# A one-core decode block: query table by a VectorE transpose, softmax sums by one product, the output weights loaded in another partition order

## The chip, the cores and the metric

The kernel runs on one core of one Trainium2 chip. The metric is the device time of one execution in microseconds (us); lower is better. The kernel before has a median of 1302.57 us in 3 runs (1302.52 to 1302.81).

## The reference: what is computed

One decode step of a block with attention and a feed-forward part side by side, all in float32: 4 sequences, one new token each, 32 heads of 128, 4096 cached keys and values per head, width 512, inner width 1792.

```python
xn = _layernorm(x)                                  # x: 4 x 1 x 512
q = (xn @ wq)                                       # 4 sequences, 32 heads, 128
scores = einsum("bhqd,bhkd->bhqk", q, k_cache) * 128 ** -0.5
o = einsum("bhqk,bhkd->bhqd", softmax(scores), v_cache)
out = x + o.reshape(4, 1, 4096) @ wo + silu(xn @ w1) @ w2
```

The two caches hold 268 MB each, so 561 MB are read from memory for a few thousand numbers of output.

## The kernel before

**Loads.** All large loads are issued by SyncE (SP) and go through one queue, in the order of the program: w1, wq, then k and v alternately, then wo in two halves and w2 in five pieces (function `load`, L161 to L165; issues L168 to L323). Only x (by ScalarE, L169) and the result (L527) go through another queue. There are three large buffers in SBUF of 64 KB per partition: `kb[0]`, `kb[1]` and `vb`. The keys of a step go to `kb[0]` and `kb[1]` in turn, the values to `vb`. The early weights lie in buffers that are not yet needed: w1 and the work space of the layer norm in `kb[1]`, wq in `vb`. At the end wo lies in `vb` and w2 in `kb[1]`. SP waits before an issue until the buffer is free: `k_free` comes from ScalarE when it has read the scores of a step, `v_free` from TensorE when it has collected the output of a step.

**Start.** VectorE computes the layer norm over the 4 rows of x (L190 to L219). TensorE transposes the result into `xpad` (L252), multiplies it with w1 (L259) and, when wq has landed, with wq (L273). The 4 column groups of TensorE work at the same time; each computes the queries of 8 heads for 4 sequences, with 32 output rows of which 4 are used. The query table `q_col` holds for each of the 32 steps (one sequence, 4 heads) a column of 128 numbers per head. It is made by scaling `ps_q` into `q_all` (L279), 32 products with a selection matrix `heads` (L286) and a copy (L295). The first load of v needs the buffer of wq and waits for the products with wq (`p_q`, L306).

**Steps.** 32 steps, two per loop iteration (L342 to L432). In each, VectorE multiplies the keys with the query (L358), GpSimd and VectorE add up the products (L378, L353), ScalarE takes the exponentials (L390) and leaves their sums per partition in `sums`, TensorE multiplies the weights with the values (L408) and collects the output into `o_t` (L419).

**End.** With the last step done, VectorE spreads `sums` over a selection matrix `quad` (L444), four products with `ones` give the softmax sums (L455), their reciprocals are taken (L461), `o_t` is transposed in blocks (L464), a product with the permutation `perm` puts rows in the order of wo (L468), and the result is scaled into `xo` (L474). Then come 32 products with wo (L487), one for each of the 32 rows that a partition holds, and 7 with w2 (L493), all into `ow`, again with 4 column groups; ScalarE copies `ow` to `os` (L498). Four more rows of w2 are multiplied with another arrangement (`accumulate`, L237 to L243: the 512 output columns are cut into 4 blocks of 128, one for each column group, into `acc`), then `os` is added to `acc` by a product with `pick` (L505), then two rows of w2, then the last row in two halves (L508 to L525). The input x had been added to `acc` by products at the start (L247). The result goes out by L527.

wo is loaded with `wo.rearrange("(p r) n -> p r n")`: partition p gets rows 32 p to 32 p + 31, the first 16 of them by the first load and the others by the second.

## Time and profile before

| | |
|---|---|
| median of 3 runs | 1302.57 us |
| the profiled execution: its own time | 1303.4 us |
| the profiled execution: span from first to last instruction | 1300.5 us |
| bytes moved by DMA | 561.07 MB, mean 431 GB/s |
| busy: VectorE 964.9, GpSimd 580.9, TensorE 361.1, ScalarE 110.2 us | 74%, 45%, 28%, 8% of the span |
| mean granted TensorE clock | 0.623 |

In the rows of the profile, L12 is line 12 of the kernel. DVE is VectorE, PE is TensorE's products and PEld its weight loads, ACT is ScalarE, POOL is GpSimd, SP is SyncE, and a name with a q (SPq) is that engine's sequencer. A row of the timeline has the start in us, the busy time in us, engine, line, operation, output and input, and the number of instructions merged in it; in brackets stands how long the engine was idle before it and what ended that. The tiles that share a buffer are shown under the buffer's name, `k` for `kb[0]` and `kb[1]` and `v` for `vb`, so w1 and w2 land in `k` and wq and wo in `v`. A float32 product is carried out as two passes and counts two records.

### The profile page before, as it was taken

What the parts mean: (1) busy time and instruction counts of PE and PEld (TensorE: products, weight loads), DVE (VectorE), ACT (ScalarE), POOL (GpSimd) and SP (SyncE); (2) the same over time, 40 slices, a digit from 0 to 9 for tenths busy, and PEclk for the clock granted to TensorE, in tenths of its full rate; (3) what the DMA queues carried; (4) which work ended last, traced back from release to release, by engine and by line L of the source; (5) the groups of instructions that cost most, each with busy time, mean ns of one, the idle gap of its engine ahead of it and who ended that gap; (6) DMA issues with size and microseconds to landing.
All of it is one profiled execution on the core that took longest, in us unless ns stands there. A gap on an engine that the chain in (4) does not pass through costs nothing. (4 is left out here: it accounts for less than half of the span.)

```text
span 1300.5 us, 7378 instructions
## 1 busy us (share of the span) xinstructions
PE 361.1 (28%) x2628; PEld 113.3 (9%) x2628; DVE 964.9 (74%) x449; ACT 110.2 (8%) x311; POOL 580.9 (45%) x137
## 2 busy tenths in 40 slices
PE   2221233321233221123322132332123332113337
PEld 0100001000000000000000000100000000001002
DVE  2499877887777887777797777788777788777770
ACT  1010101001010100101000010100101010010100
POOL 0255534554444554443555443455444455444350
PEclk8755666655666655666665566665566665566668
DMA  9999999999999999999999999999999999999998
GB/s 403 450 422 440 429 441 427 435 435 423 447 423 447 423 445 425 441 429 439 427 437 433 425 445 423 447 423 447 423 443 427 439 429 441 427 431 439 423 433 358
DMA packets 10533, 561.07 MB, mean 431 GB/s; under 512 B 1176, under 2 KB 1432, under 8 KB 1568
## 3 DMA queue, kind: packets, MB, share of 16 engines
q1 hardware_dynamic: 10512, 560.99, 99.6%
q8 instruction: 3, 0.05, 0.0%
q10 hardware_dynamic: 16, 0.02, 0.0%
q14 instruction: 2, 0.02, 0.0%
HBM read 561.00 MB, written 0.01 MB: 431 GB/s over the span
## 5 line engine op out<-in xcount | busy, mean ns | idle before, releaser
L378 POOL TENSOR_TENSOR k<-k 128x2048 f32<-128x2048 f32 x128 | 578.7, 4532 | 676.8 <-POOLq L326 676.8
L358 DVE TENSOR_TENSOR k<-k,q_b 128x4096 f32<-128x4096 f32 x128 | 562.4, 4414 | 226.2 <-DVEq L326 226.1
L408 PE MATMUL o_ps<-v,p_t 128*16 128x512 f32 x1984 | 285.0, 739 | 867.1 <-PEq L326 867.1
L353 DVE TENSOR_REDUCE s<-k 128x32 f32<-128x2048 f32 x128 | 290.8, 2272 | 17.9 <-DVEq L326 17.9
L408 PEld LDWEIGHTS o_ps<-v,p_t 128*16 128x16 f32 x1984 | 67.1, 113 | 1059.2 <-issue 1059.2
L398 ACT ACTIVATE o_sb<-o_ps 128x512 f32<-128x512 f32 x32 | 19.1, 597 | 1010.2 <-ACTq L326 1010.2
L329 DVE COPY q_of<-q_col 128x4 f32 (+1 forms) x33 | 84.8, 2571 | 0.0
L390 ACT ACTIVATE p_t<-s,gm 32x128 f32<-32x128 f32 x128 | 65.9, 515 | 46.0 <-ACTq L326 43.9
L419 PE MATMUL o_t<-pick,o_sb 128*128 128x4 f32 x256 | 33.6, 254 | 33.3 <-PEq L326 33.3
L419 PEld LDWEIGHTS o_t<-pick,o_sb 128*128 128x128 f32 x256 | 31.0, 191 | 62.6 <-issue 62.6
L390 ACT ACT_TABLE_LOAD x16 | 20.5, 1283 | 98.4 <-ACTq L326 98.4
L390 ACT ACTIVATION_READ_ACCUMULATOR p_t<-s,gm x128 | 24.9, 195 | 0.0
L279 DVE TENSOR_SCALAR q_all<-ps_q 128x1024 f32<-128x1024 f32 x1 | 1.2, 1224 | 20.6 <-PE ps_q L273 20.6
L444 DVE TENSOR_TENSOR k<-sums,quad 128x512 f32<-128x512 f32 x1 | 0.7, 693 | 19.0 <-PE o_t L419 19.0
L333 DVE STREAM_TRANSPOSE q_b<-q_of 128x128 f32<-128x128 f32 x33 | 10.8, 327 | 4.9
L367 DVE TENSOR_REDUCE m<-s 128x1 f32<-128x128 f32 x32 | 9.2, 286 | 4.7
L273 PE MATMUL ps_q<-v,xpad 128*32 128x512 f32 x64 | 8.8, 706 | 13.3 <-DMA v<-in_A_wq_dram 13.3
L408 PE MATMUL o_ps<-k,p_t 128*16 128x512 f32 x64 | 9.5, 757 | 8.3 <-DMA k<-in_A_v_cache_dram 8.3
L369 DVE STREAM_TRANSPOSE mt<-m 128x32 f32<-128x32 f32 x32 | 6.8, 212 | 4.7
L522 DVE COPY k<-acc 4x128 f32<-4x128 f32 x2 | 0.6, 286 | 12.5 <-PE acc L239 12.5
L371 DVE TENSOR_REDUCE gm<-mt 128x1 f32<-128x32 f32 x32 | 6.0, 186 | 4.7
L267 DVE STREAM_TRANSPOSE hT<-k 128x448 f32<-128x448 f32 x1 | 0.9, 939 | 10.3 <-ACT k L265 10.3
(62 smaller groups left out, 54.1 us busy)
## 6 DMA issues: line engine op xcount, KB each, us to landing
v<-in_A_wo_dram SPq DMA_DIRECT2D x2, 4096.0 KB, 27.2
k<-in_B_w_dram SPq DMA_DIRECT2D x1, 3584.0 KB, 11.2
k<-in_B_w_dram SPq DMA_DIRECT2D x1, 1792.0 KB, 30.3
k<-in_B_w_dram SPq DMA_DIRECT2D x1, 1024.0 KB, 32.4
k<-in_A_k_cache_dram SPq DMA_DIRECT2D x32, 45.4
k<-in_B_w_dram SPq DMA_DIRECT2D x1, 512.0 KB, 33.2
v<-in_A_v_cache_dram SPq DMA_DIRECT2D x31, 27.2
k<-in_B_w_dram SPq DMA_DIRECT2D x2, 128.0 KB, 33.0
```

The source lines that it names most:

```text
L273: t = nc.tensor.matmul(ps_q[32 * j : 32 * j + 32, u, :], xpad[:, c, :], wq_t[:, c, h * Dh : (h + G) * Dh], start=(c == 0), stop=(c == DC - 1),
L329: nc.vector.tensor_copy(q_of, q_col[:, at, :].rearrange("p i g -> p (i g)")).then_inc(spread_done, 1)
L333: nc.vector.transpose(q_b[:, n, :], q_of[:, :, None].to_broadcast([P, G, PH])).then_inc(spread_done, 1)
L353: nc.vector.tensor_reduce(s[:, a:z], k[:, a:z, : Dh // 2], axis=AX, op=ALU.add).then_inc(summed, 1)
L358: nc.vector.tensor_tensor(k[:, a:z, :], k[:, a:z, :], q_b[:, n, None, :].to_broadcast([P, z - a, Dh]), op=ALU.mult,).then_inc(products, 1)
L367: nc.vector.tensor_reduce(m_t, s, axis=AX, op=ALU.min).then_inc(summed, 1)
L369: nc.vector.transpose(mt, m_t.to_broadcast([P, PH])).then_inc(summed, 1)
L378: nc.gpsimd.tensor_tensor(kb[n][:, a:z, : Dh // 2], kb[n][:, a:z, : Dh // 2], kb[n][:, a:z, Dh // 2 :], op=ALU.add,).then_inc(halves, 1)
L390: t = nc.scalar.activation(p_t[rows, :, g], s_t[n][rows, :], AF.Exp, bias=gm[n][rows, :], scale=-1.0, accum_out=sums[rows, bass.ds(i * 2 + ...
L398: nc.scalar.activation(o_sb.rearrange("p r d -> p (r d)"), o_ps, AF.Copy).then_inc(rows_ready, 1)
L408: t = nc.tensor.matmul(o_ps[j : j + NR * G, :], p_t[:, rows, :].rearrange("p r g -> p (r g)"), v[:, rows, :].rearrange("p r d -> p (r d)") ...
L419: t = nc.tensor.matmul(to, o_sb[:, r, :], pick[:, r * G : (r + 1) * G], start=(r == 0), stop=(r == NR - 1),)
```

## The change

1. **Query table.** The products with wq are arranged so that column group j computes head 4 n + j, and not 8 j + n: only the columns of `wq_t` that a product takes change. One VectorE transpose in blocks of 32 x 32 takes `ps_q` (128 x 1024) to `q_t`, which lies in `vb` over wq, and one VectorE instruction scales it into `q_col`. `q_all`, `heads` and their 32 products are gone. The first load of v now waits for `d_col`, since `q_t` is in its buffer.
2. **Softmax sums.** `lt` is 128 x 128 instead of 128 x 512, `ones` is 128 x 128, and one product gives every sum in the place where `o_t` has the number to be divided. VectorE takes the reciprocal, multiplies, and transposes into `xo`. The product with `perm` is gone, and so is the clearing of `xo`.
3. **wo.** The transpose leaves the heads in another order over the partitions. wo is loaded in that order: partition 32 q + h gets rows 128 h + 32 q to 128 h + 32 q + 31. Each partition still gets 16 rows of 512 by the first load and 16 by the second, and each is one run of 32 KB in memory. The products take 4 columns of `xo` and not 32.
4. **x.** x lies in rows 8 to 11 of a cleared tile of 32 rows, `x_sb`; its load waits for the clearing. The layer norm is over 32 rows. Before the steps, VectorE copies `x_sb` into the first 32 rows of `ow` and clears the others; `add_x` takes rows 8 to 11 with the sums. The 4 products that added x to `acc` are gone.
5. **w2.** 12 rows instead of 7 go into `ow`; the copy `os` is after all of these; one row is left for `acc`, then `os`, then the last row. The second load of w2 has 5 rows and not 4, the third 1 and not 2.

```diff
-W2_CUTS = (7, 11)
+W2_CUTS = (7, 12)
+X_ROW = 8
...
-        got_x = load(act, "x", x_sb, xf)
+        c_x = dve.done(nc.vector.memset(x_sb, 0.0))
+        got_x = load(act, "x", x_sb[X_ROW : X_ROW + B], xf, c_x)
...
-        pe.wait(c_ident, got_x)
-        accumulate(ident[:B, :B], x_sb, start=True)
...
+        wq_g = wq_t.rearrange("p c (n g d) -> p c n g d", g=G, d=Dh)
...
-                        wq_t[:, c, h * Dh : (h + G) * Dh], start=(c == 0), stop=(c == DC - 1),
+                        wq_g[:, c, G * u : G * u + G, j, :], start=(c == 0), stop=(c == DC - 1),
...
-        d_q = dve.done(nc.vector.tensor_scalar_mul(
-                q_all.rearrange("p u g d -> p (u g d)"), ps_q.rearrange("p u n -> p (u n)"), -scale,
-            ))
-        pe.wait(d_q, d_pick)
-        for g in range(G):
-            for a in range(4):
-                for u in range(NQ):
-                    t = nc.tensor.matmul(
-                        ps_b[32 * g : 32 * g + 32, 32 * a : 32 * a + 32],
...
+        d_qt = dve.done(
+            nc.vector.transpose(q_t, ps_q.rearrange("p u (m e) -> p (u m) e", e=PH))
+        )
+        dve.wait(d_qt)
         d_col = dve.done(
-            nc.vector.tensor_copy(q_col[:, :T, :], ps_b.rearrange("p (a i) -> p i a", a=4))
-        )
+            nc.vector.tensor_scalar_mul(
+                q_col[:, :T, :].rearrange("p (n b) a -> p n b a", b=B),
+                q_t.rearrange("p (n a) e -> p n e a", a=G)[:, :, :B, :], -scale,
+            )
+        )
+
+        nc.vector.tensor_copy(ow[:PH], x_sb)
+        nc.vector.memset(ow[PH : 2 * PH], 0.0)
+        d_ow = dve.done(nc.vector.memset(ow[2 * PH :], 0.0))
...
-            load(sp, "v", vb, cache(v_cache, i), p_q if i == 0 else (v_free, i))
+            load(sp, "v", vb, cache(v_cache, i), d_col if i == 0 else (v_free, i))
...
-        wo_p = wo.rearrange("(p r) n -> p r n", p=P)
+        wo_p = wo.rearrange("(h q r) n -> q h r n", q=4, r=PH)
...
-            got_wo.append(load(sp, name, wo_t[:, a:z], wo_p[:, a:z], (v_free, T - 1)))
+            got_wo.append(load(sp, name, wo_t[:, a:z], wo_p[:, :, a:z], (v_free, T - 1)))
...
+        p_l = pe.done(
+            nc.tensor.matmul(
+                ps_b, ones, lt.rearrange("p t g -> p (t g)"), start=True, stop=True
+            )
+        )
         dve.wait(p_l)
...
+        t = dve.done(nc.vector.reciprocal(rl.rearrange("p t g -> p (t g)"), ps_b))
+        dve.wait(t, p_o)
+        t = dve.done(nc.vector.tensor_tensor(o_n, o_t, rl, op=ALU.mult))
+        dve.wait(t)
         d_x = dve.done(
...
+            nc.vector.transpose(xo, o_n.rearrange("p (n b) g -> p b n g", b=B))
+        )
...
-                    ow[j : j + 32, :], xo[:, r, :], wo_t[:, r, :], start=(r < 4), stop=False
+                    ow[j : j + B, :], xo[:, :, r], wo_t[:, r, :], start=(r < 4), stop=False
...
+        rows = f_edges[-2]
+        for n, (a, z) in enumerate(zip(f_edges[:-2], f_edges[1:-1])):
+            pe.wait(got_w2[n])
+            for f in range(a, z):
+                j = 32 * (f % 4)
+                t = nc.tensor.matmul(
+                    ow[j : j + B, :], hT[:, f, :B], w2_t[:, f, :], start=False,
+                    stop=(f >= rows - 4),
+                )
         act.wait(pe.done(t))
         a_os = act.done(nc.scalar.activation(os, ow, AF.Copy))
...
+        pe.wait(got_w2[-1])
+        for f in range(rows, f_edges[-1]):
+            accumulate(hT[:, f, :B], w2_t[:, f, :], start=(f == rows))
+        pe.wait(a_os, d_add)
+        accumulate(add_x, os)
```

Three places in the order of the instructions. First SP at the end of its program, behind the last load of keys or values; `k` and `v` are the buffers, and the shape is that of the destination, partitions first. Before:

```order
L163 DMA k_90<-in_A_v_cache_dram 128x16384
L163 DMA v<-in_A_wo_dram 128x8192 x2
L163 DMA k_91<-in_B_w_dram 128x3584
L163 DMA k_91<-in_B_w_dram 128x2048
L163 DMA k_91<-in_B_w_dram 128x1024
L163 DMA k_91<-in_B_w_dram 128x256 x2
```

In the change:

```order
L164 DMA k_88<-in_A_v_cache_dram 128x16384
L164 DMA v<-in_A_wo_dram 128x1x8192 x2
L164 DMA k_89<-in_B_w_dram 128x3584
L164 DMA k_89<-in_B_w_dram 128x2560
L164 DMA k_89<-in_B_w_dram 128x512
L164 DMA k_89<-in_B_w_dram 128x256 x2
```

The order of the loads is the same; the two loads of wo have a dimension more (their source is now 4 x 32 x 8192 numbers, where it was 128 x 8192), and the second and third load of w2 have other sizes.

Second TensorE at the end of its program, behind the last step: the products for the softmax sums and the permutation, then wo (input `v`), then w2 with `hT`. Before:

```order
L455 MATMUL ps_a<-ones,k_91 128x1 x4
L468 MATMUL ps_b<-k_91,perm 128x128
L487 MATMUL ps_q<-v,k_91 32x512 x32
L493 MATMUL ps_q<-k_91,hT 32x512 x7
L239 MATMUL acc<-k_91,hT 4x128 x16
L239 MATMUL acc<-k_91,pick 4x128 x4
L239 MATMUL acc<-k_91,hT 4x128 x12
```

In the change:

```order
L441 MATMUL ps_b<-k_89,ones 128x128
L461 MATMUL ps_q<-v,k_89 4x512 x32
L470 MATMUL ps_q<-k_89,hT 4x512 x12
L237 MATMUL acc<-k_89,hT 4x128 x4
L237 MATMUL acc<-k_89,add_x 4x128 x4
L237 MATMUL acc<-k_89,hT 4x128 x4
```

The sum of `ow` and `acc` (`pick` before, `add_x` now) had 12 products behind it and now has 4, and five rows of w2 that were behind ScalarE's copy of `ow` are ahead of it.

Third VectorE between the layer norm and the first step: `hT` is the feed-forward part, `q_col` the query table, and the last two rows spread the first query. Before:

```order
L267 STREAM_TRANSPOSE hT<-k_91 128x448
L279 TENSOR_SCALAR q_all<-ps_q 128x1024
L295 COPY q_col<-ps_b 128x128
L329 COPY q_of<-q_col 128x4
L333 STREAM_TRANSPOSE q_b<-q_of 128x128
```

In the change:

```order
L263 STREAM_TRANSPOSE hT<-k_89 128x448
L276 STREAM_TRANSPOSE v<-ps_q 128x1024
L280 TENSOR_SCALAR q_col<-v 128x128
L286 COPY ps_q<-x_sb 32x512
L287 MEMSET ps_q 32x512
L288 MEMSET ps_q 64x512
L321 COPY q_of<-q_col 128x4
L325 STREAM_TRANSPOSE q_b<-q_of 128x128
```

The transpose and the scaling stand where the scaling and the copy stood, and three writes into `ow` (the memory of `ps_q`) stand ahead of the first query.

More of the change, by code (lines that the diff above doesn't have):

```diff
@@ L93 @@
     hT = small([P, FC, PH], "hT")
-    q_all = small([P, NQ, G, Dh], "q_all")
-    heads = small([P, NQ, 4, NQ, B], "heads")
+    x_sb = small([PH, D], "x_sb")
     q_col = small([P, T + 1, G], "q_col")
@@ L101 @@
     pick = small([P, NR * G], "pick")
-    quad = small([P, G, 4], "quad")
-    perm = small([P, P], "perm")
-    ones = small([P, 1], "ones")
-    rl = small([P, B], "rl")
-    nmean = small([B, 1], "nmean")
-    var = small([B, 1], "var")
-    rstd = small([B, 1], "rstd")
-    t1 = small([B, 1], "t1")
+    add_x = small([P, B], "add_x")
+    quad = small([P, G], "quad")
+    ones = small([P, P], "ones")
+    nmean = small([PH, 1], "nmean")
+    var = small([PH, 1], "var")
+    rstd = small([PH, 1], "rstd")
+    t1 = small([PH, 1], "t1")
     small([P, -(CONST_AT + taken) % 256 // 4 + 64], "fill")
@@ L125 @@
     at = DC * F
-    x_sb, xc, sq, xn = (early[:B, at + n * D : at + (n + 1) * D] for n in range(4))
-    h_sb = early[:, at + 4 * D : at + 4 * D + FJ]
+    xc, sq, xn = (early[:PH, at + n * D : at + (n + 1) * D] for n in range(3))
+    h_sb = early[:, at + 3 * D : at + 3 * D + FJ]
     wq_t = vb.rearrange("p (c m) d -> p c (m d)", c=DC)
+    q_t = vb.rearrange("p r d -> p (r d)")[:, : T * PH].rearrange("p (m e) -> p m e", e=PH)
     wo_t = vb.rearrange("p r d -> p (r d)").rearrange("p (r n) -> p r n", n=D)
@@ L131 @@
     w2_t = late[:, : FC * D].rearrange("p (f n) -> p f n", f=FC)
-    lt = late[:, FC * D : (FC + 1) * D].rearrange("p (b n g) -> p b n g", b=B, n=N)
-    y_t = late[:, (FC + 1) * D : (FC + 1) * D + P].rearrange("p (b h) -> p b h", b=B)
-    xo = late[:, (FC + 4) * D : (FC + 4) * D + PH * PH].rearrange("p (r m) -> p r m", r=PH)
+    lt = late[:, FC * D : FC * D + T * G].rearrange("p (t g) -> p t g", g=G)
+    rl = late[:, FC * D + P : FC * D + 2 * P].rearrange("p (t g) -> p t g", g=G)
+    o_n = late[:, FC * D + 2 * P : FC * D + 3 * P].rearrange("p (t g) -> p t g", g=G)
+    xo = late[:, (FC + 1) * D : (FC + 1) * D + B * PH].rearrange("p (b r) -> p b r", b=B)
     ow = ps_q[:, 0, :]
@@ L185 @@
         nc.vector.memset(q_col[:, T:, :], 0.0).then_inc(s_free, 1)
-        nc.vector.memset(heads, 0.0)
         c_ops = dve.done(nc.vector.memset(o_ps, 0.0))
@@ L223 @@
         )
-        nc.vector.tensor_copy(perm, ident.rearrange("p (q h) -> p h q", q=4))
-        for u in range(NQ):
-            t = nc.vector.tensor_copy(
-                heads[:, u, :, u, :], ident.rearrange("p (j e) -> p j e", j=4)[:, :, :B]
-            )
         d_pick = dve.done(
             nc.vector.tensor_reduce(
-                quad,
-                ident.rearrange("p (g m) -> p g m", g=G)[:, :, None, :].to_broadcast([P, G, 4, PH]),
-                axis=AX, op=ALU.add,
-            )
+                quad, ident.rearrange("p (g m) -> p g m", g=G), axis=AX, op=ALU.add,
+            )
+        )
+        dve.wait(d_pick)
+        d_add = dve.done(
+            nc.vector.tensor_add(add_x, pick[:, :B], ident[:, X_ROW : X_ROW + B])
         )
@@ L243, in accumulate @@
             return last
-        pe.wait(c_ident, got_x)
-        accumulate(ident[:B, :B], x_sb, start=True)
-        pe.wait(d_xn)
-        xt = ps_b[:, : DC * B].rearrange("p (c b) -> p c b", c=DC)
+        pe.wait(c_ident, d_xn)
+        xt = ps_b.rearrange("p (c b) -> p c b", c=DC)
         xn_c = xn.rearrange("b (p c) -> b c p", c=DC)
         for c in range(DC):
-            t = nc.tensor.transpose(xt[:, c, :], xn_c[:, c, :], ident[:B, :B])
+            t = nc.tensor.transpose(xt[:, c, :], xn_c[:, c, :], ident[:PH, :PH])
         p_xt = pe.done(t)
         dve.wait(p_xt)
-        d_xpad = dve.done(nc.vector.tensor_copy(xpad[:, :, :B], xt))
+        d_xpad = dve.done(nc.vector.tensor_copy(xpad[:, :, :B], xt[:, :, X_ROW : X_ROW + B]))
         pe.wait(d_xpad, got_w1)
@@ L271 @@
                 for u in range(NQ):
-                    h = HJ * j + G * u
                     t = nc.tensor.matmul(
                         ps_q[32 * j : 32 * j + 32, u, :], xpad[:, c, :],
-                        wq_t[:, c, h * Dh : (h + G) * Dh], start=(c == 0), stop=(c == DC - 1),
+                        wq_g[:, c, G * u : G * u + G, j, :], start=(c == 0), stop=(c == DC - 1),
                     )
@@ L278 @@
         dve.wait(p_q)
-        d_q = dve.done(nc.vector.tensor_scalar_mul(
-                q_all.rearrange("p u g d -> p (u g d)"), ps_q.rearrange("p u n -> p (u n)"), -scale,
-            ))
-        pe.wait(d_q, d_pick)
-        for g in range(G):
-            for a in range(4):
-                for u in range(NQ):
-                    t = nc.tensor.matmul(
-                        ps_b[32 * g : 32 * g + 32, 32 * a : 32 * a + 32],
-                        q_all[:, u, g, 32 * a : 32 * a + 32],
-                        heads[:, u].rearrange("p j v b -> p (j v b)"),
-                        start=(u == 0), stop=(u == NQ - 1),
-                    )
-        p_col = pe.done(t)
-        dve.wait(p_col)
+        d_qt = dve.done(
+            nc.vector.transpose(q_t, ps_q.rearrange("p u (m e) -> p (u m) e", e=PH))
+        )
+        dve.wait(d_qt)
         d_col = dve.done(
-            nc.vector.tensor_copy(q_col[:, :T, :], ps_b.rearrange("p (a i) -> p i a", a=4))
-        )
+            nc.vector.tensor_scalar_mul(
+                q_col[:, :T, :].rearrange("p (n b) a -> p n b a", b=B),
+                q_t.rearrange("p (n a) e -> p n e a", a=G)[:, :, :B, :], -scale,
+            )
+        )
+        nc.vector.tensor_copy(ow[:PH], x_sb)
+        nc.vector.memset(ow[PH : 2 * PH], 0.0)
+        d_ow = dve.done(nc.vector.memset(ow[2 * PH :], 0.0))
         got_k[1] = load(sp, "k1", kb[1], cache(k_cache, 1), p_h, d_h, p_xt)
@@ L437 @@
         p_o = v_free, T
-        pool.wait((k_free, T))
-        c_xo = pool.done(nc.gpsimd.memset(xo, 0.0))
         dve.wait((v_free, T))
@@ L444 @@
             nc.vector.tensor_tensor(
-                lt,
-                sums.rearrange("p (n b) -> p b n", b=B)[:, :, :, None].to_broadcast([P, B, N, G * 4]),
-                quad.rearrange("p g q -> p (g q)")[:, None, None, :].to_broadcast(
-                    [P, B, N, G * 4]
-                ),
-                op=ALU.mult,
+                lt, sums[:, :, None].to_broadcast([P, T, G]),
+                quad[:, None, :].to_broadcast([P, T, G]), op=ALU.mult,
             )
@@ L453 @@
         pe.wait(d_lt)
-        for b in range(B):
-            t = nc.tensor.matmul(
-                ps_a[:, b : b + 1],
-                lt[:, b].rearrange("p n g -> p (n g)"), ones, start=True, stop=True,
-            )
-        p_l = pe.done(t)
-        dve.wait(p_l)
-        d_rl = dve.done(nc.vector.reciprocal(rl, ps_a[:, :B]))
-        dve.wait(p_o)
-        d_y = dve.done(
-            nc.vector.transpose(y_t, o_t.rearrange("p (n b) g -> p b n g", b=B))
-        )
-        pe.wait(d_y)
-        p_x = pe.done(
+        p_l = pe.done(
             nc.tensor.matmul(
-                ps_b, perm, y_t.rearrange("p b r -> p (b r)"), start=True, stop=True,
+                ps_b, ones, lt.rearrange("p t g -> p (t g)"), start=True, stop=True
             )
         )
-        dve.wait(p_x, d_rl, c_xo)
+        dve.wait(p_l)
+        t = dve.done(nc.vector.reciprocal(rl.rearrange("p t g -> p (t g)"), ps_b))
+        dve.wait(t, p_o)
+        t = dve.done(nc.vector.tensor_tensor(o_n, o_t, rl, op=ALU.mult))
+        dve.wait(t)
         d_x = dve.done(
-            nc.vector.tensor_tensor(
-                xo[:, :, :B], ps_b.rearrange("p (b r) -> p r b", b=B),
-                rl[:, None, :].to_broadcast([P, PH, B]), op=ALU.mult,
-            )
+            nc.vector.transpose(xo, o_n.rearrange("p (n b) g -> p b n g", b=B))
         )
-        pe.wait(d_x)
+        pe.wait(d_x, d_ow)
         for n, (a, z) in enumerate(zip(edges[:-1], edges[1:])):
@@ L487 @@
                 nc.tensor.matmul(
-                    ow[j : j + 32, :], xo[:, r, :], wo_t[:, r, :], start=(r < 4), stop=False
+                    ow[j : j + B, :], xo[:, :, r], wo_t[:, r, :], start=(r < 4), stop=False
                 )
-        pe.wait(d_h, got_w2[0])
-        for f in range(f_edges[1]):
-            j = 32 * (f % 4)
-            t = nc.tensor.matmul(
-                ow[j : j + 32, :], hT[:, f, :], w2_t[:, f, :], start=False,
-                stop=(f >= f_edges[1] - 4),
-            )
+        pe.wait(d_h)
+        rows = f_edges[-2]
[7 more added lines that the diff above has]
+                )
         act.wait(pe.done(t))
         a_os = act.done(nc.scalar.activation(os, ow, AF.Copy))
-        for n, (a, z) in enumerate(zip(f_edges[1:-1], f_edges[2:])):
-            pe.wait(got_w2[n + 1])
-            for f in range(a, z):
-                accumulate(hT[:, f, :B], w2_t[:, f, :])
-            if n == 0:
-                pe.wait(a_os)
-                accumulate(pick[:, :B], os)
+        pe.wait(got_w2[-1])
[3 more added lines that the diff above has]
+        accumulate(add_x, os)
         for n, side in enumerate(sides):
```

## The prediction

> **What bounds the kernel now.** I read the slices of the page first, to see whether one resource is busy from end to end, and the packets below them.

> ```profile
> DMA  9999999999999999999999999999999999999998
> GB/s 403 450 422 440 429 441 427 435 435 423 447 423 447 423 445 425 441 429 439 427 437 433 425 445 423 447 423 447 423 443 427 439 429 441 427 431 439 423 433 358
> DMA packets 10533, 561.07 MB, mean 431 GB/s; under 512 B 1176, under 2 KB 1432, under 8 KB 1568
> ## 3 DMA queue, kind: packets, MB, share of 16 engines
> q1 hardware_dynamic: 10512, 560.99, 99.6%
> ...
> q10 hardware_dynamic: 16, 0.02, 0.0%
> ```

> The DMA engines are busy in every slice. So a compute instruction saved is worth something only where the DMA waits for it, and behind the last transfer. The chain of waits says the same of the end:

> ```profile
> 1262.59 32.40 DMA k<-in_B_w_dram
> 1294.99 0.04 issue
> 1295.03 2.12 PE acc L239 x60
> ```

> The end waits for w2, at the back of the one queue. What lies ahead of it is in the timeline and in the list of DMA issues (time from issue to landing in the last column):

> ```profile
> 1224.88 0.33 SPq L163 DMA_DIRECT2D k<-in_A_v_cache_dram  x1
> ...
> 1260.72 0.80 SPq L163 DMA_DIRECT2D v<-in_A_wo_dram  x2
> ...
> 1262.21 2.23 SPq L163 DMA_DIRECT2D k<-in_B_w_dram  x5
> ```

> ```profile
> v<-in_A_wo_dram SPq DMA_DIRECT2D x2, 4096.0 KB, 27.2
> ...
> k<-in_B_w_dram SPq DMA_DIRECT2D x2, 128.0 KB, 33.0
> ...
> k<-in_A_v_cache_dram SPq DMA_DIRECT2D x1, 44.1
> ```

> The last values land at 1224.88 + 44.1 = 1269.0. Behind them stand wo (8.39 MB) and w2 (1792 x 512 numbers, 3.67 MB): 12.06 MB at the mean 431 GB/s are 28.0 us, which gives 1297.0. The last piece of w2 is issued at the end of the row of 1262.21, at about 1264.0, and lands 33.0 us later: 1297.0 too. The queue is full to the end, at 431 / 16 = 26.9 GB/s for each engine, and what lies behind it is some 3.5 us of the span.

> **The change part by part.** The profiled execution took 1303.4 us: 1300.5 of span and 2.9 around it. It is 0.8 us above the median, to which I carry the differences.

> *wo, the term that decides.* The bytes and the runs of 32 KB are the same, the shape of the transfer is not: its source was 128 x 8192 numbers and is now 4 x 32 x 8192. What the outer dimension does can be read from the packets. Queue q1 carries 73 transfers (w1, wq, 32 of keys, 32 of values, 2 of wo, 5 of w2), each of 128 outer rows: 73 x 128 = 9344 packets of data. 10512 - 9344 = 1168 = 73 x 16 are left: every such transfer ends with 16 small packets, one for each engine that took part. Queue q10 carries two transfers of 4 outer rows (x and the result): 16 packets, 8 of them data, so 4 small ones each. The count under 512 B agrees: 1168 + 8 = 1176. So a transfer of 4 outer rows ran on 4 engines, and one of 128 on 16. [...] I take **4 engines**.

> [...]

> The price: 8.39 MB over 4 engines are 2.097 MB each, at 26.9 GB/s 77.9 us, where 16 engines take 19.5: **58.4 us** more. Twelve engines go on to w2 and are done early, but the other four hold a sixteenth of each piece behind their wo: 3.67 / 16 = 0.229 MB, 8.5 us. So w2 is complete at 1269.0 + 77.9 + 8.5 = 1355.4, and nothing in the program can use the idle twelve.

> The unknown is the rate of an engine when four work alone. No row shows it. On one side, the fastest slice of the row GB/s has 450, 4% above the mean: 77.9 would be 74.6, 3.3 us less. On the other, 26.9 GB/s may belong not to the engine but to its way into a group of partitions, and then two engines that write by the same way get 13.5 each. That is the third rival. I take 26.9, since the runs of 32 KB are nearest to those of 64 KB that go at it.

> *The end behind the loads.* The rows of before:

> ```profile
> 1280.47 0.69 DVE L444 TENSOR_TENSOR k<-sums,quad 128x512 f32<-128x512 f32 x1 [19.01 <-PE o_t L419]
> ...
> 1283.56 0.79 PE L468 MATMUL ps_b<-k,perm 128*128 128x128 f32 x2 [0.48 <-DVE k L464]
> 1284.39 0.29 DVE L474 TENSOR_TENSOR k<-ps_b,rl 128x128 f32<-128x128 f32 x1 [0.88 <-PE ps_b L468]
> ...
> 1293.03 1.89 PE L493 MATMUL ps_q<-k,hT 128*32 128x512 f32 x14
> ...
> 1294.98 0.60 ACT L498 ACTIVATE k<-ps_q 128x512 f32<-128x512 f32 x1 [15.71 <-PE ps_q L493]
> ...
> 1295.91 0.40 PE L239 MATMUL acc<-k,pick 128*4 128x128 f32 x8
> ...
> 1296.29 1.02 PE L239 MATMUL acc<-k,hT 128*4 128x128 f32 x24
> ```

> From 1280.47 to 1284.39 + 0.29 the softmax sums and the permutation take 4.21 us. The new chain is four VectorE instructions of 128 x 128 at 0.29 (the row of L474) and one product at 0.79 (L468), with four gaps of some 0.1 between (an estimate from the 0.04 between the rows of L468 and L474 and the 0.48 ahead of L468): about 2.4 us, so 1.8 less. I count it as nothing: the second half of wo would land at 1269.0 + 77.9 = 1346.9, over 60 us later. If wo came as before it would still be nothing, because the copy of `ow` then waits for w2's second piece.

> The new order of w2 costs a little. Before, w2's second piece (4 rows) lands at 1294.99 and its products need no copy behind them; the copy of `ow` ran at 1294.98, beside them. Now the piece has 5 rows, 0.26 MB more, 0.6 us later: 1295.6 in the old count. Its 10 records at 1.89 / 14 us are 1.35: 1296.95. ScalarE's copy with 0.06 ahead of it and 0.60: 1297.6. The product with `add_x`, 0.1 later, 0.40: 1298.1. Then 8 records at 1.02 / 24: 0.3, so 1298.4, where the chain of before leaves TensorE at 1295.03 + 2.12 = 1297.15. That is **+1.2 us**: the sum of `ow` had 12 products behind it and is now itself behind the last but one piece. The narrower weights of the products with wo are worth nothing, since those products wait for wo.

> *The start.* Everything there lies beside loads that are issued already:

> ```profile
> 8.39 0.17 DVE L255 COPY xpad<-ps_b 128x16 f32<-128x16 f32 x1
> 18.89 0.94 DVE L267 STREAM_TRANSPOSE hT<-k 128x448 f32<-128x448 f32 x1 [10.32 <-ACT k L265]
> 40.38 1.22 DVE L279 TENSOR_SCALAR q_all<-ps_q 128x1024 f32<-128x1024 f32 x1 [20.55 <-PE ps_q L273]
> ...
> 43.94 0.17 DVE L329 COPY q_of<-q_col 128x4 f32<-128x4 f32 x1
> ...
> 52.05 8.75 DVE L358 TENSOR_TENSOR k<-k,q_b 128x4096 f32<-128x4096 f32 x2 [7.47 <-DVEq L326]
> ```

> The table took from 40.38 to 43.94, 3.56 us. The transpose of 1024 columns, at 0.94 for 448, is 2.15, the scaling of 128 x 128 between the 0.29 of L474 and the 1.22 of L279; I take 0.3, so 2.5 us. The three writes into `ow` have 512 columns each, at half of L279's 1.22: 1.8 us, with both ends 0.9 and 3.7. So the first query is ready between 0.2 us earlier and 3.5 later, and VectorE waited 7.47 us there for the first keys. SP now waits for `d_col` with the first values and with every later load behind it, and issues them 2.5 us later than at 40.4; the queue then still holds the keys of steps 0 and 1, of which the first are used only at 52.05. x lands later by its clearing and perhaps by w1 and wq ahead of it. Its chain ends at 8.39 + 0.17, its result is next used by VectorE at 18.89, and SP needs that for the keys of step 1, with those of step 0 in the queue until 52: over 30 us are free. All this is nothing while the queue is full; without that cover it would be at most the 3.5 us. The loop itself is unchanged.

> The sum: 1303.4 + 58.4 + 1.2 = 1363.0 for the profiled execution, 1302.57 + 59.6 = **1362.2 us** for the median.

> **The rivals.**

> *All 16 engines carry wo* (the side that is not slower). If the shares are made along the destination's 128 partitions, wo takes its 19.5 us and only the end's 1.2 are left: 1303.8. For it: the destination's shape is that of before, and the bytes in memory are as long. Against it: the transfers of 4 rows took 4 engines, and a share of the source must then cut through its outer dimension. It decides as soon as the shares come from the destination alone; there is nothing between. 10%.

> *The early end helps.* If wo came as before and the end were bound by the softmax chain and not by w2, its 1.8 us would come off: 1302.57 - 1.8 = 1300.8. Against it stand the chain of waits, in which TensorE's last products start 0.04 us after w2's landing, and the new place of the copy. 2%.

> *Two engines share a way in.* Each of the four engines gets a block of 32 neighbouring partitions and walks through it in the same order. If the way into SBUF is shared by partitions of two blocks, then engines that walk in step get half of 26.9: wo takes 155.7 us, 136.2 more than before, and the time is 1302.57 + 136.2 + 1.2 = 1440.0. Where they get out of step it falls towards 1362.2. For it: in the trace 16 engines share the partitions evenly and reach about the same rate in every slice, so that engine and way in cannot be told apart. Against it: no row shows an engine below its 26.9 for another's sake. 38%.

> [...]

> **How the numbers follow.** Four engines at full rate 48%, shared ways 38%, 16 engines 10%, the early end 2%, and 2% for a mishap outside these. The forecast is 1362.2. With shared ways and the engines out of step for part of the time, all between it and 1440 can come, so the range holds both: from 1362.2 less 3.3 (rate) and 1.2 (no cost at the end), 1357.7, rounded to 1357, up to 1440.0 plus the 6 us that w2's other shares, 8.5 us of the twelve engines, could take from the same ways: 1446. That leaves out the 16 engines, the early end and the mishap, 14%. Faster by over 0.2% (2.6 us, about what a measurement of this kernel can tell from no change) needs the early end and more: 1%. Within 0.2% are the 16 engines and the rest of the early end: 11%. Slower: 88%.

> **What would show it.** Packets on q1 10488 and under 512 B 1152 (two transfers with 4 small packets and not 16) show the four engines; 10512 and 1176 show sixteen and make the prediction wrong. The first half of wo then lands about 47 us after its issue (8.3 to 1269.0, then half of 77.9) and the second 86, where the two had 27.2 in the middle; with shared ways 86 and 164. The rate should fall to 4 x 26.9 = 108 GB/s from some 1278 on, or to 54 with shared ways. The wait of TensorE in the middle of wo should be the longest of the end. The copy of `ow` should stand between w2's products and `add_x`. If the first step starts later than 52.05, the start was not hidden.

## The result and the profile after

The changed kernel takes 1423.37 us (1422.12 to 1425.4, 5 runs) against 1302.57: ratio 1.093, interval 1.0917 to 1.0942, 120.8 us slower. Forecast were 1362.2, in a range from 1357 to 1446. The direction and the place were right, the size of one term was not. The page of the changed kernel, its slices and its packets:

```profile
DMA  9999999999999999999999999999999999993221
GB/s 419 423 441 435 422 441 441 424 435 441 437 420 441 441 424 435 441 437 420 443 439 426 433 441 437 420 443 439 430 430 441 437 420 443 439 330 85 68 68 59
DMA packets 10509, 561.07 MB, mean 395 GB/s; under 512 B 1152, under 2 KB 1408, under 8 KB 1544
## 3 DMA queue, kind: packets, MB, share of 16 engines
q1 hardware_dynamic: 10488, 560.99, 92.6%
...
q10 hardware_dynamic: 16, 0.02, 0.0%
```

Up to slice 35 nothing has changed. From slice 37 on the DMA's share falls to three tenths and less. The packets on q1 are 10488 and those under 512 B 1152, 24 fewer each: two transfers close with 4 small packets in place of 16. wo went through 4 engines.

TensorE at the end of the changed kernel (L400 multiplies the last values, L461 is wo, L470 and L237 are w2 and the sum):

```profile
1270.27 8.61 PE L400 MATMUL o_ps<-k,p_t 128*16 128x512 f32 x64 [9.84 <-DMA k<-in_A_v_cache_dram]
...
1344.07 5.81 PE L461 MATMUL ps_q<-v,k 128*4 128x512 f32 x32 [62.39 <-DMA v<-in_A_wo_dram]
1407.77 6.38 PE L461 MATMUL ps_q<-v,k 128*4 128x512 f32 x32 [57.89 <-DMA v<-in_A_wo_dram]
1413.98 2.81 PE L470 MATMUL ps_q<-k,hT 128*4 128x512 f32 x24
1416.55 0.46 PE L237 MATMUL acc<-k,hT 128*4 128x128 f32 x8
1417.48 0.40 PE L237 MATMUL acc<-k,add_x 128*4 128x128 f32 x8 [0.47 <-ACT k L475]
```

It waits 62.39 us for the first half of wo and 57.89 for the second, which is there at 1407.8. Counted from 1270.3, when the last values have landed, wo's 8.39 MB took 137.5 us: 61.0 GB/s, 15.3 for each of the four engines (the 14.9 in the expectations below is counted from some 3 us earlier, when the first engines are through with the values). The stretches of the changed kernel (busy time of PE, PEld, DVE, ACT and POOL, the clock, the DMA's share of 16 engines, and GB/s):

```profile
1290.00:1310.00 20.00, 0.00 (x0) 0.00 (x0) 0.00 (x0) 0.00 (x0) 0.00 (x0) 0.50 0.28 67
1310.00:1330.00 20.00, 0.00 (x0) 0.00 (x0) 0.00 (x0) 0.00 (x0) 0.00 (x0) 0.50 0.29 71
1330.00:1350.00 20.00, 5.81 (x32) 1.02 (x32) 0.00 (x0) 0.00 (x0) 0.00 (x0) 0.54 0.25 64
...
1390.00:1407.00 17.00, 0.00 (x0) 0.00 (x0) 0.00 (x0) 0.00 (x0) 0.00 (x0) 0.50 0.24 76
```

A share of 0.25 is 4 engines of 16, busy without a gap. But they move 64 to 76 GB/s, 16 to 19 each, where each moved 26.9 before. So two things are to be explained: that there are four, and that each is slow.

### The profile page after: what moved, and what is told of

Same layout as the page of the kernel before. It is cut to its first block, busy times and chain, and to the rows that moved or that the text cites. A ratio compares the mean times of both kernels' runs of the same rounds, so it can differ in the third digit from the quotient of the medians.

```text
span 1421.5 us, 7157 instructions
## 1 busy us (share of the span) xinstructions
PE 357.4 (25%) x2518; PEld 108.3 (8%) x2518; DVE 966.6 (68%) x450; ACT 110.2 (8%) x311; POOL 579.9 (41%) x136
## 2 busy tenths in 40 slices
DMA packets 10509, 561.07 MB, mean 395 GB/s; under 512 B 1152, under 2 KB 1408, under 8 KB 1544
## 3 DMA queue, kind: packets, MB, share of 16 engines
q1 hardware_dynamic: 10488, 560.99, 92.6%
## 5 line engine op out<-in xcount | busy, mean ns | idle before, releaser
L400 PE MATMUL o_ps<-v,p_t 128*16 128x512 f32 x1984 | 284.7, 738 | 870.7 <-PEq L318 870.7
L400 PEld LDWEIGHTS o_ps<-v,p_t 128*16 128x16 f32 x1984 | 67.1, 113 | 1063.2 <-issue 1063.2
L382 ACT ACTIVATE p_t<-s,gm 32x128 f32<-32x128 f32 x128 | 65.9, 515 | 46.1 <-ACTq L318 44.1
L461 PE MATMUL ps_q<-v,k 128*4 128x512 f32 x64 | 12.2, 931 | 120.3 <-DMA v<-in_A_wo_dram 120.3
L461 PEld LDWEIGHTS ps_q<-v,k 128*4 128x4 f32 x64 | 2.1, 116 | 129.5 <-issue 70.6
L400 PE MATMUL o_ps<-k,p_t 128*16 128x512 f32 x64 | 8.6, 698 | 9.8 <-DMA k<-in_A_v_cache_dram 9.8
## 6 DMA issues: line engine op xcount, KB each, us to landing
v<-in_A_wo_dram SPq DMA_DIRECT2D x2, 4096.0 KB
v<-in_A_v_cache_dram SPq DMA_DIRECT2D x31, 27.2
k<-in_B_w_dram SPq DMA_DIRECT2D x2, 128.0 KB, 108.1
```

Source lines behind the costliest of these rows:

```text
L382: t = nc.scalar.activation(p_t[rows, :, g], s_t[n][rows, :], AF.Exp, bias=gm[n][rows, :], scale=-1.0, accum_out=sums[rows, bass.ds(i * 2 + ...
L400: t = nc.tensor.matmul(o_ps[j : j + NR * G, :], p_t[:, rows, :].rearrange("p r g -> p (r g)"), v[:, rows, :].rearrange("p r d -> p (r d)") ...
L461: nc.tensor.matmul(ow[j : j + B, :], xo[:, :, r], wo_t[:, r, :], start=(r < 4), stop=False)
```

## The experiments

Three theories for the slow engines. **Shared ways**: partitions that differ by 32 have one way into SBUF, the four engines walk through blocks of 32 partitions in the same order, and two that are at the same row get half each. (That each engine takes one block of neighbouring rows is an assumption: no view shows which partition an engine writes.) **Few engines**: an engine is slower when only four work. **Strides**: runs 256 KB apart in memory are read more slowly. Ahead of them stands the question whether it is wo alone.

**e1_wo_order_alone.** The kernel before, with the load of wo alone changed.

```diff
-        wo_p = wo.rearrange("(p r) n -> p r n", p=P)
+        wo_p = wo.rearrange("(h q r) n -> q h r n", q=4, r=PH)
...
-            got_wo.append(load(sp, name, wo_t[:, a:z], wo_p[:, a:z], (v_free, T - 1)))
+            got_wo.append(load(sp, name, wo_t[:, a:z], wo_p[:, :, a:z], (v_free, T - 1)))
```

> The kernel before with nothing changed but the shape and order of wo's two loads (source 4 x 32 x 8192 numbers). The rows of wo then meet other heads than the reference has, so the output is another. If wo's load is the whole loss but for the 1.2 us that the new end was priced at, the time is 1302.6 + 120.8 - 1.2 = 1422 us, with 10488 packets on q1 and 1152 under 512 B. Rival: the other edits carry part of the loss (the end, the start, the late x); each us that they carry is missing here, and if they carry half it is about 1362.

1419.98 us, ratio 1.0911 (1.0894 to 1.0928), with the 10488 and 1152 packets. The load of wo is 117 of the 121 us by itself.

**e2_wo_natural.** The other way round: the changed kernel with the two lines above taken back.

> The changed kernel with wo loaded in the order of before (128 x 8192 on both sides); xo is still in the transpose's order, so heads meet other rows of wo than in the reference. If wo's load is the whole loss but for the end: 1303.8 us (1302.6 + 1.2 for the second piece of w2 with the copy behind it), 10512 packets on q1. Rival: the early end of the softmax chain helps once wo is back: 1300.8. Rival: other edits carry part of the loss: 1310 or more.

1304.49 us, ratio 1.0013 (1.0004 to 1.0022): 1.8 us over before, nearer to the 1.2 of the end than to the rivals. TensorE at its end:

```profile
1296.29 1.45 PE L470 MATMUL ps_q<-k,hT 128*4 128x512 f32 x9 [1.17 <-DMA k<-in_B_w_dram]
1297.15 0.40 PE L237 MATMUL acc<-k,hT 128*4 128x128 f32 x6
1297.58 0.59 PE L470 MATMUL ps_q<-k,hT 128*4 128x512 f32 x1
1298.01 0.38 PE L237 MATMUL acc<-k,hT 128*4 128x128 f32 x2
1298.86 0.40 PE L237 MATMUL acc<-k,add_x 128*4 128x128 f32 x8 [0.47 <-ACT k L475]
```

The product with `add_x` waits for ScalarE's copy, as foretold. The five rows take from 1296.29 to 1298.17, 1.9 us and not 1.35: rows 7 and 11 go to the same column group, and the last record runs by itself. That is half a us, most of the 0.6 by which 1.8 exceeds the forecast; that the column group is the reason is read from the rows, no run separates it.

**e3_four_apart.** Four engines, but no two of them at partitions 32 apart.

```diff
-        wo_p = wo.rearrange("(h q r) n -> q h r n", q=4, r=PH)
+        wo_p = wo.rearrange("(h j q r) n -> q j h r n", q=4, j=4, r=PH)
...
-            got_wo.append(load(sp, name, wo_t[:, a:z], wo_p[:, :, a:z], (v_free, T - 1)))
+            for q in range(4):
+                got = load(sp, name, wo_t[32 * q : 32 * q + 32, a:z], wo_p[q][:, :, a:z], (v_free, T - 1))
+            got_wo.append(got)
```

> The changed kernel with each half of wo loaded by four transfers, one for each block of 32 partitions, each with a source of 4 x 8 x 8192 numbers: still four engines, still runs of 32 KB, but the engines now write 8 neighbouring partitions each and no two of them write partitions that are 32 apart at the same time. Rows come in another order, so the output is another. Shared ways into SBUF: an engine gets its full 26.9 GB/s, wo takes 77.9 us, 1362 us in all. Rival, an engine is slower when only four work: still 14.9 GB/s, 1423. Rival, the strides in memory slow the reading: the strides are longer here (1 MB from run to run, 256 KB before), so 1423 or more.

1369.22 us, ratio 1.0511 (1.0495 to 1.0527). Its packets on q1 are 10512: eight transfers of wo that close with 4 small packets each make as many as two that close with 16, so four engines carried them. The stretches and wo's products:

```profile
1290.00:1300.00 10.00, 0.00 (x0) 0.00 (x0) 0.00 (x0) 0.00 (x0) 0.00 (x0) 0.50 0.33 120
1300.00:1310.00 10.00, 0.00 (x0) 0.00 (x0) 0.00 (x0) 0.00 (x0) 0.00 (x0) 0.50 0.29 118
...
1340.00:1350.00 10.00, 0.00 (x0) 0.00 (x0) 0.00 (x0) 0.00 (x0) 0.00 (x0) 0.50 0.25 108
```

```profile
1268.65 9.24 PE L402 MATMUL o_ps<-k,p_t 128*16 128x512 f32 x64 [8.50 <-DMA k<-in_A_v_cache_dram]
...
1315.08 6.48 PE L463 MATMUL ps_q<-v,k 128*4 128x512 f32 x32 [34.38 <-DMA v<-in_A_wo_dram]
1353.51 6.04 PE L463 MATMUL ps_q<-v,k 128*4 128x512 f32 x32 [31.95 <-DMA v<-in_A_wo_dram]
```

The same four engines with the same share of 0.25 move 108 GB/s: 27.0 each, the full rate. Few engines is refuted, and so are the strides, which are longer here. This kernel is what the forecast priced (1362.2); the 7 us above it lie in the first half of wo, which took 46.4 us where the second took 38.4 (half of 77.9 is 39.0). Beside the first half the other twelve engines write w2. That they meet there is argued, not shown; the trace's record of each packet fits it, since 37 of the 39 packets of wo that took over 1.30 us are in the first half.

**e6_near_rows.** The strides by themselves: four engines, blocks of 32 partitions as in the change, runs 64 KB apart.

```diff
-            got_wo.append(load(sp, name, wo_t[:, a:z], wo_p[:, :, a:z], (v_free, T - 1)))
+            near = bass.AP(
+                wo.tensor, a * D, [[30 * PH * D, 4], [PH * D, 32], [1, (z - a) * D]]
+            )
+            got_wo.append(load(sp, name, wo_t[:, a:z], near, (v_free, T - 1)))
```

> The changed kernel with the same four engines and the same blocks of 32 partitions, but each engine reads runs 64 KB apart as before the change, and not 256 KB (blocks overlap by two runs, so the data are not wo's and the output is another). Shared ways: nothing changes, 1418 to 1440 by how far the engines get out of step. Rival, the strides in memory: 1362 to 1369.

1422.25 us, ratio 1.0919 (1.0903 to 1.0936): no change.

```profile
1290.00:1310.00 20.00, 0.00 (x0) 0.00 (x0) 0.00 (x0) 0.00 (x0) 0.00 (x0) 0.50 0.29 69
1310.00:1330.00 20.00, 0.00 (x0) 0.00 (x0) 0.00 (x0) 0.00 (x0) 0.00 (x0) 0.50 0.29 71
```

**e5_two_engines.** Half the engines: the source is cut in two (`q=2`, 64 rows each), so that one writes partitions 0 to 63 and one 64 to 127.

```diff
-        wo_p = wo.rearrange("(h q r) n -> q h r n", q=4, r=PH)
+        wo_p = wo.rearrange("(h q r) n -> q h r n", q=2, r=PH)
```

> The changed kernel with wo's source cut in 2 x 64 x 8192 numbers: two engines, one writing partitions 0 to 63 and the other 64 to 127; the output is another, since rows come in another order. Shared ways: no two engines meet now, so each has its full 26.9 to 27.5 GB/s (the four transfers on four engines gave 108 to 118 GB/s over four); wo takes 152 to 156 us, 133 to 136 more than before: 1302.6 + 134 + 1.8 = 1438, hardly above the four engines that meet. Rival, the strides slow the reading and an engine reads at the 14.9 GB/s of the changed kernel: 281 us, 1566.

1445.17 us, ratio 1.1096 (1.1079 to 1.1113): two engines are 22 us slower than four, and 7 us above what was expected: the halves of wo came 81.0 and 79.7 us after what lay ahead of them, 160.7 in all and not 152 to 156. The stretches in which only these two work show each at its full rate, a share of 0.12 to 0.13 with 53 to 54 GB/s, although, by the same assumption, they walk through partitions 64 apart at the same time:

```profile
1390.00:1410.00 20.00, 0.00 (x0) 0.00 (x0) 0.00 (x0) 0.00 (x0) 0.00 (x0) 0.50 0.13 54
1410.00:1430.00 20.00, 0.67 (x4) 0.12 (x8) 0.00 (x0) 0.00 (x0) 0.00 (x0) 0.50 0.12 53
```

**e11_offset.** The four engines of the change, put out of step by loads of data that nothing reads; no row of wo goes another way than in the change.

```diff
+        wo_f = wo.rearrange("(p r) n -> p (r n)", r=4)
+        spare = [
+            load(sp, "d0", free[:17], wo_f[:17], (k_free, T)),
+            load(sp, "d1", late[:51, 28 * D : 32 * D], wo_f[:51]),
+        ]
```

> The changed kernel with two loads more ahead of wo, of data that nothing reads: 17 runs of 8 KB on one engine, then 51 on three (17 each). Engine 0 comes 10.4 us late to wo, engines 1 and 2 5.2 us, engine 3 not at all; so each of two that walk through blocks 32 apart is more than 4 rows of 32 KB (4.85 us) from the other, and should never meet it. The output is the reference's. If meeting in step is the cause: full rate, 1302.6 + 58.4 + 10.4 + 1.8 = 1373, perhaps 6 more as in the four transfers on four engines: 1373 to 1380, some 45 us faster than the changed kernel although it loads more. Rival, the engines share something whatever row they are at: 1423 + 10 = 1433.

1379.34 us, ratio 1.0584 (1.0567 to 1.0602): 44 us faster than the changed kernel, with 0.56 MB more to load.

```profile
1310.00:1330.00 20.00, 3.97 (x20) 0.81 (x24) 0.00 (x0) 0.00 (x0) 0.00 (x0) 0.50 0.28 117
1330.00:1350.00 20.00, 1.59 (x16) 0.21 (x8) 0.00 (x0) 0.00 (x0) 0.00 (x0) 0.67 0.25 110
```

110 GB/s at a share of 0.25, where the changed kernel has 64 in the same stretch. The engines are slow because they are at the same row at the same time; shared ways stands.

**e4_blocks.** A repair that was tried: 16 engines, the same rows in the same partitions, one transfer for each block of 32.

```diff
-            got_wo.append(load(sp, name, wo_t[:, a:z], wo_p[:, :, a:z], (v_free, T - 1)))
+            for q in range(4):
+                got = load(sp, name, wo_t[32 * q : 32 * q + 32, a:z], wo_p[q][:, a:z], (v_free, T - 1))
+            got_wo.append(got)
```

> The changed kernel with the same rows of wo in the same partitions, but each half loaded by four transfers of 32 partitions each, 32 x 8192 numbers on both sides: 16 engines with 2 rows each; the output is the reference's. Shared ways: 32 partitions are reached by 8 ways and so two engines meet on each: 13.5 GB/s each, wo takes 38.9 us, 19.5 more than before, 1302.6 + 19.5 + 1.2 = 1323; if engines get out of step less. Rival, an engine is slower when few work: full rate, 1303.8. Rival, the strides slow the reading: 14.9 GB/s each as in the changed kernel, 35 us, 1319; that one is told apart by the four transfers on four engines, not here.

1326.56 us, ratio 1.0185 (1.0169 to 1.0201).

```profile
1270.00:1280.00 10.00, 8.79 (x69) 2.33 (x69) 0.00 (x0) 0.60 (x1) 0.00 (x0) 0.85 1.02 215
1280.00:1290.00 10.00, 1.07 (x8) 0.79 (x7) 1.85 (x4) 0.00 (x0) 0.00 (x0) 0.66 1.00 210
```

All 16 engines are busy (1.00) and move half as much as before: 210 GB/s, 13.1 each. The share alone would call this a full DMA; the row of GB/s tells that it is not.

**e7_two_queues.** The same blocks, those for partitions 64 to 127 issued by GpSimd on its own queue, so that both sides could be written at once.

```diff
-            got_wo.append(load(sp, name, wo_t[:, a:z], wo_p[:, :, a:z], (v_free, T - 1)))
+            for q in range(2):
+                got = load(sp, name, wo_t[32 * q : 32 * q + 32, a:z], wo_p[q][:, a:z], (v_free, T - 1))
+            got_wo.append(got)
...
+            for q in (2, 3):
+                got = load(pool, name, wo_t[32 * q : 32 * q + 32, a:z], wo_p[q][:, a:z], (v_free, T - 1))
+            got_odd.append(got)
```

> The changed kernel with wo in transfers of 32 partitions on 16 engines, where SP issues those for partitions 0 to 63 and GpSimd, on a queue of its own, those for 64 to 127 at the same time; the output is the reference's. Shared ways: the engines have packets for both sets of ways, so most of the 19.5 us of the blocks on one queue come back: 1304.5 (the end's 1.8 alone) to 1312. Rival, the engines take the two queues' packets in step, so that all write the same side: 1326 as with one queue.

1328.04 us, ratio 1.0191 (1.0175 to 1.0206): my expectation fell, nothing came back.

```profile
1280.00:1285.00 5.00, 5.00 (x36) 1.03 (x32) 0.00 (x0) 0.00 (x0) 0.00 (x0) 0.71 1.01 216
1285.00:1290.00 5.00, 3.71 (x33) 1.71 (x26) 0.29 (x1) 0.60 (x1) 0.00 (x0) 0.97 1.02 220
```

That fits the rival, all engines changing sides in step, but the profile does not show which partition an engine writes. The run is also no clean test: GpSimd's loads were issued from 1262.0 on, beside the last values, and these landed at 1277.8 and not at 1270.3 as in the changed kernel, so both sides of wo were in flight together for a part of the time only. The cause stays open.

**e8_perm_back.** The version to which this points: wo and w2's cuts as before, the product with `perm` back, the rest as changed.

```diff
-W2_CUTS = (7, 12)
+W2_CUTS = (7, 11)
...
-        wo_p = wo.rearrange("(h q r) n -> q h r n", q=4, r=PH)
+        wo_p = wo.rearrange("(p r) n -> p r n", p=P)
...
+        p_x = pe.done(nc.tensor.matmul(ps_a[:, :P], perm, y_t, start=True, stop=True))
+        dve.wait(p_x)
+        d_x = dve.done(
+            nc.vector.tensor_copy(xo.rearrange("p b r -> p (b r)"), ps_a[:, :P])
+        )
```

> The changed kernel with wo's load of before, the permuting product put back behind the transpose (one product and one copy more on a path of 1.2 us, ahead of wo's products), and w2's cuts of before (7 rows in ow, the copy beside the 4 of the second piece); query table, softmax sums and x as changed; the output is the reference's. If only wo's load and w2's new cuts cost, the time is that of before within 0.2 us: 1302.6. If the longer chain ahead of wo counts it is up to 1.5 us more; if the early chain is worth something it is below 1302.4.

1302.59 us against 1302.58, ratio 1.0 (0.9991 to 1.0009). Its TensorE at the end:

```profile
1295.18 1.06 PE L240 MATMUL acc<-k,hT 128*4 128x128 f32 x32 [0.56 <-DMA k<-in_B_w_dram]
1296.06 0.40 PE L240 MATMUL acc<-k,add_x 128*4 128x128 f32 x8
1296.39 1.01 PE L240 MATMUL acc<-k,hT 128*4 128x128 f32 x24
```

`add_x` no longer waits. So w2's new cuts cost about 1.8 us (the product with `perm`, put back beside them, can only have cost something), and query table, softmax sums and x together cost and gain nothing that the interval (1.2 us to either side) would show. No version was faster than the kernel before.

**e9_halves and e10_middle.** Which partitions share? From e8, wo in transfers of 64 partitions, or with the middle 64 together:

```diff
-            got_wo.append(load(sp, name, wo_t[:, a:z], wo_p[:, a:z], (v_free, T - 1)))
+            for lo, hi in ((0, 64), (64, 128)):
+                got = load(sp, name, wo_t[lo:hi, a:z], wo_p[lo:hi, a:z], (v_free, T - 1))
+            got_wo.append(got)
```

(e10_middle has `((32, 96), (0, 32), (96, 128))`.)

> The version with the permuting product back and wo in the order of before (1302.6), each half of wo loaded by two transfers of 64 partitions, 0 to 63 and 64 to 127: 16 engines with 4 neighbouring partitions each; the output is the reference's. Shared ways, partitions that differ by 32 having one: engines 0 and 8 meet, and so on, 13.4 GB/s each, wo takes 38.9 us: 1302.6 + 19.5 = 1322. Rival, only a group of 4 neighbouring partitions has a way of its own, 32 groups: no two engines meet, 1302.6.

> The same, but each half by three transfers: partitions 32 to 95 (16 engines), 0 to 31 and 96 to 127 (16 engines with 2 partitions each); the output is the reference's. Shared ways, partitions that differ by 32 having one and 0 to 63 other ways than 64 to 127: the middle transfer meets nothing and goes at full rate (9.7 us for its half of the bytes), the others at half (19.5): 1302.6 + 9.7 = 1312. Rival, any 64 neighbouring partitions have 8 ways: 1322. Rival, groups of 4 have ways of their own: the two outer transfers still have two engines in a group: 1312 as well; the two halves tell that one apart.

e9_halves 1325.64 us, ratio 1.0178 (1.0161 to 1.0195); e10_middle 1316.50, ratio 1.0105 (1.0088 to 1.0122). The stretches of e9_halves:

```profile
1280.00:1290.00 10.00, 2.00 (x12) 1.56 (x12) 2.14 (x5) 0.42 (x1) 0.00 (x0) 0.73 1.01 210
1290.00:1300.00 10.00, 5.49 (x32) 1.00 (x32) 0.00 (x0) 0.00 (x0) 0.00 (x0) 0.76 1.01 210
```

64 neighbouring partitions have the 210 GB/s of 32, although e9 reads the same runs of wo in memory as the kernel before: the loss is not on the side of the memory. Groups of 4 with ways of their own are refuted by e9; that any 64 have only 8 ways is refuted by e10, which is 9.1 us faster with the same number of bytes (9.7 expected). Both are some 4 us above their expectation (3.6 and 4.5), at the seams between the transfers or elsewhere; that was not followed up.

**e12_halves_offset.** e9 with engines 0 to 7 put behind by loads that nothing reads.

```diff
+        for i in range(7):
+            m = slice(8 * i, 8 * i + 8)
+            spare = [load(sp, "d0", late[m, 22 * D : 32 * D], wo_f[m, : 10 * D], (k_free, T))]
```

> The two halves of 64 partitions (1325.6) with seven loads more ahead of wo, of data that nothing reads: 20 KB each on engines 0 to 7, 143 KB or 5.3 us for each of them. Engines 0 to 7 then write the low half while 8 to 15 are at the high one. The output is the reference's. If meeting is the cause: full rate, 1302.6 + 5.3 = 1308, and up to 4 more at the seams. Rival, a transfer of 64 partitions is slow whatever the others do: 1325.6 + 5 = 1331.

1348.05 us, ratio 1.0343 (1.0326 to 1.036): outside both expectations. The spare loads go to 8 neighbouring partitions at a time, and were slow themselves:

```profile
1270.00:1275.00 5.00, 2.70 (x16) 0.66 (x20) 0.00 (x0) 0.00 (x0) 0.00 (x0) 0.50 1.11 116
1275.00:1280.00 5.00, 5.00 (x40) 1.06 (x33) 0.00 (x0) 0.00 (x0) 0.00 (x0) 0.72 0.90 93
```

A spare packet of 20 KB took 1.3 to 3.6 us by the trace's record of each packet, with a median of 2.7, where 26.9 GB/s would be 0.76. So the delay was not the 5.3 us that the test needs, and it tells nothing of the two theories.

## Why the prediction was right or wrong

**What bounds the kernel: right.** With wo as before the queue is full to the end and query table, softmax sums and x do not move the time (e8, 1302.59 us against 1302.58); in the changed kernel the end waits for wo (62.39 and 57.89 us).

**Four engines: right.** 10488 and 1152 packets, as forecast. Before, only x and the result showed 4 outer rows on 4 engines; the change and e1 show it for a source of 4 x 32 x 8192 and a destination of 128 partitions, and the trace's record of each packet has 4 packets of 32 KB under way at a time where it had 16. By what rule the number follows from the shape is not shown. Two runs show other sizes: in e5, with a source of 2, the share of 0.12 to 0.13 is two engines of 16, and e11's 10560 packets are 10488, 68 runs and 4 closing ones, which fits one engine for 17 rows and three for 51.

**The price of wo: wrong, and this is the step that failed.** "I take 26.9, since the runs of 32 KB are nearest to those of 64 KB that go at it." The second half was to be there at 1346.9 and came at 1407.8, 60.9 us later; the whole miss is 61.2. The rows of before could not show it, since there all 16 engines have 26.9 and none is slowed by another; of the two ends that I had, the third rival (13.5 GB/s, 1440.0) was the nearer. What the runs put in its place: full rate for four engines that do not meet (108 GB/s, e3; 110, e11), half for engines that meet always (210 GB/s over 16, e4), and 64 to 76 over four in the change, between the two. At 16.8 GB/s each (67 over four) they would have met for most of the time and not all.

The trace also has the time of every packet, and wo's 256 packets of 32 KB say it one by one. Before, 255 of them take 1.21 us each, which is 27.0 GB/s. In e4 and e9 none takes less than 1.9 us and the median is 2.56, about half the rate. In the changed kernel the median is 2.46 in the first quarter of the packets (with w2 beside them, up to 3.86), then 2.42, 1.97 and 1.86, and only 24 packets take 1.30 or less. By that the engines met nearly always at first and less and less later. Why they drift apart is not shown; that they are fast when apart is (in e11 224 packets take 1.30 or less).

**The signs.** One came out otherwise: the wait in the middle of wo (57.89 us) is not the longest of the end, the one ahead of its first half is (62.39). The first half took 73.8 us and the second 63.7; as in e3, w2 went beside the first. The range had allowed for that with 6 us.

**The end: right in mechanism, 1.2 us forecast, 1.8 measured** (e2 against before; e8 puts it on w2's cuts). The softmax chain was priced at 2.4 us and took from 1280.85 to 1283.35 (2.5), and was worth nothing, as forecast. That its sum fits is luck in part: the reciprocal took 0.96 us and not 0.29, the product 0.49 and not 0.79, and the gaps were shorter.

**The start: right, hidden.** VectorE there, in the changed kernel:

```profile
40.15 1.25 DVE L276 STREAM_TRANSPOSE v<-ps_q 128x1024 f32<-128x1024 f32 x1 [20.03 <-PE ps_q L269]
41.43 0.27 DVE L280 TENSOR_SCALAR q_col<-v 128x128 f32<-128x128 f32 x1
41.61 0.68 DVE L286 COPY ps_q<-x_sb 32x512 f32<-32x512 f32 x1
...
51.98 8.75 DVE L350 TENSOR_TENSOR k<-k,q_b 128x4096 f32<-128x4096 f32 x2 [7.87 <-DVEq L318]
```

The transpose took 1.25 us and not 2.15, so the table was ready sooner than priced. The first step starts at 51.98, against 52.05.

**The rivals.** 16 engines, and the early end behind it, did not come. The third rival, with 38%, is the one that the runs bear out (four engines move 64 to 76 GB/s in step and 110 out of it, e11); I gave the larger chance to the end of the price that the rows showed, though the rows showed it only for 16 engines that write all 128 partitions.

## What to carry to other kernels

The outer dimension of a load's source set how many engines carried it here (4 in the change, 2 in e5, and by e11's packets 3 and 1): before an order in memory is changed to save a product, count the closing packets of a transfer of that shape. Then ask which partitions are written at the same moment: here transfers of 32 or of 64 neighbouring partitions in one half (0 to 63 or 64 to 127) moved 210 GB/s where the loads of all 128 before moved 431 in the mean, and a DMA share of 1.00 with half the GB/s is what that looks like (e4, e9). In this kernel, bound by one full queue, instructions saved beside it were worth nothing that could be measured (e8, 1302.59 us against 1302.58), and the last pieces of the queue should have as little behind them as possible (w2's new cuts cost 1.8 us).

## What was not expected of the hardware

SP's issues in the changed kernel:

```profile
1260.46 1.29 SPq L164 DMA_DIRECT2D v<-in_A_wo_dram  x2
1262.16 54.89 SPq L164 DMA_DIRECT2D k<-in_B_w_dram  x5
```

The five issues of w2 took 54.89 us, before 2.23. They are as long in other runs in which few engines carry wo (46.67 in e3, 58.26 in e11, 111.20 with the two engines of e5) and 2.2 to 2.8 where 16 do; so it seems that SP could not issue while the few engines were behind. I take it to have cost nothing here, since those engines set the end, but any other load behind would have been late too. And VectorE's reciprocal of 128 x 128 took 0.96 us, where the product of the same size took 0.29:

```profile
1281.72 0.96 DVE L446 RECIPROCAL k<-ps_b 128x128 f32<-128x128 f32 x1 [0.58 <-PE ps_b L441]
1282.71 0.29 DVE L448 TENSOR_TENSOR k<-o_t,k 128x128 f32<-128x128 f32 x1
```
